# r and k in three buffers loaded apart from v, conv_w later, w_sg's rows in the places of w_val and w_out2, one order for all batches

## The chip, the cores and the metric

The kernel runs on one core of a Trainium2 chip. The metric is the device time in microseconds (us) of one execution. The core has five engines that follow their own instruction streams and meet at semaphores: PE (TensorE: matmuls), ACT (ScalarE), DVE (VectorE), POOL (GpSimd) and SP (SyncE, which here issues every DMA). A DMA that SP issues waits in SP's stream for what it needs, and what stands behind it in the stream waits with it.

## The reference

Three stages, all in float32, for 4 batches of 768 tokens:

```python
# attention: 8 heads of 48, a recurrence over the 768 tokens
cur = einsum('bhd,bhe->bhde', u * kt, vt)
y[:, :, t] = einsum('bhd,bhde->bhe', rt, state + cur)
state = w * state + einsum('bhd,bhe->bhde', kt, vt)
# x: (4, 768, 384), the heads side by side
h = gelu_tanh(x @ w_in)              # 1024 columns: u (512) and v (512)
v_n = layernorm(v) * g_ln
v_s = einsum('ts,bsd->btd', w_sg, v_n) + b_sg   # over all tokens of a batch
x = x + (u * v_s) @ w_out
gate = sigmoid(causal_conv(x, conv_w))          # 5 taps
out = (gate * (x @ w_val)) @ w_out2
```

w_in, w_out, w_val, w_out2 and conv_w come as float64 and are turned into float32 on the chip.

## The kernel before

**Attention by chunks.** The 24 chunks (4 batches of 6) have 128 tokens each. For chunk i the generators give PE these tasks: T (att_T: transposes of r and of k scaled, L515), S (att_S: the scores, L536), K (att_KV: keys by values into the state, L558), Y (att_Y: transposes of dv, then state and scores into y, L591, L598, L603). Around them POOL forms dv = r·k (L494), dv·u (L497), k scaled (L475) and v·sum (L499); DVE masks the scores (L544). y goes from PSUM through ACT (x_rows, L616) into one yT buffer, by two DMAs to a scratch xd and by a third back as columns of xf (L626): the transposition into x. x is split into a high and a low part (x_parts, L654 and L658) for each third of a half of 384 tokens in batch 0, for a whole half in the others.

**The MLP tasks.** Each product of 32-bit values is three matmuls (three, L757 to L759: high·high, high·low, low·high). mlp_V(b, i) gives v for 128 tokens (9 matmuls of 512 columns), mlp_U(b, half, f) u for 384 tokens (9 matmuls of 384), mlp_SG the product with w_sg (18 of 384), mlp_O1 that with w_out (12), mlp_VAL that with w_val (9), mlp_O2 that with w_out2 (9). V(b, i) needs its part of x and the upper half of w_in; U(b, half, ·) all of that half of x; SG needs all six V of its batch and one half of w_sg.

**Who sets the order.** A planner in the program itself runs while the program is built. Two lists of generators feed PE, attention and mlp; of attention three tasks are live at a time (WA = 3), of the MLP four (WM = 4): go pulls the next task only when one of the live ones is done, and takes the first live one that is ready. choose prefers attention until its planned PE time reaches A_FIRST + 0.43 of the MLP's. Work for other engines stands in chains (chain): steps with an engine or a choice of engines, a planned duration, the tokens they take and give back, and keys they wait for (after). next_step takes the step that can start first, ties by priority, then by its end. The result is a fixed order on each engine; the durations only serve the planning. Where PE has nothing to do before 130 us of planned time, go adds small filler matmuls (L170).

**The buffers around the change.** r and k of a chunk have two buffers each (rp, kp), v two. load_chunk (L456) issues the three loads, and chain ("ld", i) lets them go when T, dv, kS, D, KV and Y of chunk i-2 are done, so Y(i-2) sets the time. The ring R has NR = 13 tiles: parts of x take three tiles per half, w_sg's six rows one each (prepare_sg), a weight that is being converted one (prepare; at most NW = 3 at once), the parts of g, x2 and of the last product the rest. prepare turns a float64 weight of 128 rows into a high and a low part: a load, a step on ACT, three on DVE, a copy and a subtraction. w_val and w_out2 have tiles of their own from the start. prepare_sg loads w_sg's rows after chunk 3's load and sums their squares on ACT; scale_w_sg (a matmul of 12 columns, L407, on PE, as a task of the MLP list) gives the scale; parts_sg writes each row's two f16 parts (L436, L444) and turns them with two DMA transposes (L439). The first half of w_sg is rows 0 to 2. load_small (L260) brings g_ln, conv_w (three DMAs, L269) and b_sg after chunk 4's load.

**The MLP's order.** For b = 0, mlp (L932) lists V(0..5), scale, then U(0,d) and U(1,d) in turn, SG(0,0..3). For the other batches it lists V(i), U(0,i) in turn and then U(1,d), SG(0,d) in turn.

Of the kernel before, what the change touches and what calls it, by code (L numbers as in the profile page):

```python
# [30 lines left out]
class Kern:  # L31
# [180 lines left out]
    def consts(self):  # L212
# [15 lines left out]
        self.rp = [self.const([P, H, 64], F32, f"rp{i}") for i in range(2)]  # L228
        self.kp = [self.const([P, H, D], F32, f"kp{i}") for i in range(2)]
# [110 lines left out]
    def prepare(self, key, rows, hi, lo, prio, after=()):  # L340
# [15 lines left out]
        def parts(f):  # L356
            return f.rearrange("p (c n) -> p c n", c=hi.shape[1]) if len(hi.shape) == 3 else f
# [42 lines left out]
    def scale_w_sg(self):  # L400
# [63 lines left out]
    def att_new(self, i):  # L464
# [717 lines left out]
```

## Time and profile before

| | us |
|---|---|
| median of 3 runs | 492.62 (490.49 to 495.46) |
| the profiled execution | 496.19 |
| its span, first to last instruction | 494.4 |
| PE busy (share of the span) | 468.7 (95%) |
| DVE busy | 348.5 (70%) |
| ACT busy | 208.3 (42%) |
| POOL busy | 175.2 (35%) |

The mean granted clock of PE over the span is 0.971 of full speed. Matmuls are pipelined and the profile models their ends, so a row's duration is longer than the distance to the next one; the pace is read from starts. The page's chain that ended last gives PE 82% of the span, DVE 5%, POOL 4%, ACT 3%, DMA 2% and 3% to waits for nothing that the profile shows.

### The profile page before, as it was taken

What the parts mean: (1) busy time and instruction counts of PE and PEld (TensorE: products, weight loads), DVE (VectorE), ACT (ScalarE), POOL (GpSimd) and SP (SyncE); (2) the same over time, 40 slices, a digit from 0 to 9 for tenths busy, and PEclk for the clock granted to TensorE, in tenths of its full rate; (3) what the DMA queues carried; (4) which work ended last, traced back from release to release, by engine and by line L of the source; (5) the groups of instructions that cost most, each with busy time, mean ns of one, the idle gap of its engine ahead of it and who ended that gap; (6) DMA issues with size and microseconds to landing.
All of it is one profiled execution on the core that took longest, in us unless ns stands there. A gap on an engine that the chain in (4) does not pass through costs nothing.

```text
span 494.4 us, 9195 instructions
## 1 busy us (share of the span) xinstructions
PE 468.7 (95%) x3550; PEld 392.1 (79%) x3550; DVE 348.5 (70%) x699; ACT 208.3 (42%) x447; POOL 175.2 (35%) x202
## 2 busy tenths in 40 slices
PE   6798797799999999999999999999999999999996
PEld 6677585597777998877788899887787888877796
DVE  5987778966798583656588587467469694667992
ACT  3547856562363435542343163634205165312232
POOL 6766467373014223654244335446101011400000
PEclk9978988899999999999999999999999999999999
DMA  8859985992301434331231451431000301000002
GB/s 158 234 126 285 200 219 123 156 213 68 81 1 50 95 72 122 81 80 34 49 65 42 120 128 34 113 80 34 2 1 16 98 16 49 0 2 0 1 33 70
DMA packets 116274, 41.39 MB, mean 84 GB/s; under 512 B 89344, under 2 KB 114048, under 8 KB 116224
## 3 DMA queue, kind: packets, MB, share of 16 engines
q1 hardware_dynamic: 116224, 40.73, 34.9%
q8 instruction: 30, 0.49, 0.4%
q14 instruction: 20, 0.16, 0.1%
HBM read 28.92 MB, written 9.44 MB: 78 GB/s over the span
## 4 chain that ended last, share of the span: by engine, by line
PE 82%; DVE 5%; POOL 4%; issue 3%; ACT 3%; DMA 2%; SPq 0%; DVEq 0%; POOLq 0%; ACTq 0%
PE pm L757 22%; PE pm L759 20%; PE pm L758 20%; PE pa L603 5%; PE pa L536 4%; PE pa L515 3%; PE pa L598 3%; PE pa L591 2%; PE pa L558 2%; POOL dv L499 1%; DVE sc L544 1%; POOL dv L494 1%; ACT junk L386 1%; DMA wsg<-psg 1%; POOL ks L475 1%
## 5 line engine op out<-in xcount | busy, mean ns | idle before, releaser
L757 PE MATMUL pm<-wsg,vh 128*128 128x384 f16 x192 | 62.9, 328 | 0.0
L759 PE MATMUL pm<-wsg,vh 128*128 128x384 f16 x192 | 62.6, 326 | 0.0
L758 PE MATMUL pm<-wsg,vh 128*128 128x384 f16 x192 | 62.6, 326 | 0.0
L876 DVE SCALAR_TENSOR_TENSOR S<-xf,cw,S 128x384 f32<-128x384 f32 x96 | 59.5, 639 | 2.5 <-ACT S L874 2.1
L844 DVE SCALAR_TENSOR_TENSOR S<-pm,gs,b_bc 128x384 f32<-128x384 f32 x32 | 19.7, 616 | 30.7 <-PE pm L759 30.6
L499 POOL TENSOR_TENSOR dv<-v,dd 128x384 f32<-128x384 f32 x24 | 26.3, 1094 | 39.5 <-DVE dd L492 39.4
L544 DVE TENSOR_TENSOR sc<-pa,mask 128x512 f32<-128x512 f32 x48 | 31.3, 684 | 12.6 <-PE pa L536 10.8
L908 POOL TENSOR_TENSOR R<-S,R 128x384 fp32r<-128x384 f32 x9 | 9.3, 1036 | 78.5 <-ACT R L1110 60.2
L573 ACT ACTIVATE T<-T,W 112x112 f32<-112x112 f32 x80 | 26.8, 380 | 20.5 <-DVE T L567 20.1
L536 PE MATMUL pa<-rT,kT 48*128 48x128 f32 x384 | 29.4, 295 | 5.9 <-ACT kT L521 3.7
L757 PE MATMUL pm<-R,win 128*128 128x384 f32 x96 | 34.9, 363 | 0.0
L757 PE MATMUL pm<-R,wout 128*128 128x384 f32 x96 | 34.2, 357 | 0.0
L536 PEld LDWEIGHTS pa<-rT,kT 48*128 48x128 f32 x384 | 24.7, 196 | 11.7 <-ACT kT L521 5.3
L757 PE MATMUL pm<-win,R 128*128 128x512 f32 x72 | 31.3, 434 | 1.9 <-ACT R L654 1.9
L783 POOL TENSOR_TENSOR rs<-rs,exps 128x1 f32<-128x1 f32 x24 | 14.0, 582 | 53.2 <-DVE rs L780 53.2
L1110 ACT CAST R<-S 128x384 fp32r<-128x384 f32 x30 | 15.4, 513 | 40.4 <-DVE S L846 23.8
L759 PE MATMUL pm<-R,win 128*128 128x384 f32 x96 | 32.3, 337 | 0.0
L759 PE MATMUL pm<-R,wout 128*128 128x384 f32 x96 | 32.3, 336 | 0.0
L758 PE MATMUL pm<-R,wout 128*128 128x384 f32 x96 | 32.3, 336 | 0.0
L758 PE MATMUL pm<-R,win 128*128 128x384 f32 x96 | 32.2, 336 | 0.0
L494 POOL TENSOR_TENSOR dv<-rp,kp 128x384 f32<-128x384 f32 x24 | 25.8, 1073 | 18.1 <-DMA kp<-in_k_dram 14.5
L796 DVE BATCH_NORM_STATS2 bst<-A 128x6 f32<-128x512 f32 x24 | 16.6, 691 | 21.0 <-ACT A L795 21.0
(166 smaller groups left out, 1254.9 us busy)
## 6 DMA issues: line engine op xcount, KB each, us to landing
rp<-in_r_dram SPq DMA_DIRECT2D x24, 192.0 KB, 3.8
kp<-in_k_dram SPq DMA_DIRECT2D x24, 192.0 KB, 3.8
v<-in_v_dram SPq DMA_DIRECT2D x24, 192.0 KB, 2.7
xd<-yT SPq DMA_DIRECT2D x48, 96.0 KB, 2.3
xf<-xd SPq DMA_DIRECT2D x24, 192.0 KB, 2.7
out_dram<-S SPq DMA_DIRECT2D x24, 192.0 KB, 2.1
Rst<-in_moe_w_in_dram SPq DMA_DIRECT2D x8, 384.0 KB, 5.2
Rst<-in_moe_w_out_dram SPq DMA_DIRECT2D x7, 384.0 KB, 5.2
```

The costliest lines, as they stand in the source:

```text
L494: self.chain(("dv", i), ("P", 956.0, lambda e: e.tensor_mul(dv, rp, kp)), after=[("ld", i)] + ([("dT", i - 2)] if i > 1 else []), prio=pr(i))
L499: ("P", 788.0, lambda e: e.tensor_mul(dv, self.vt[i], x["dd"].unsqueeze(2).to_broadcast([P, H, D]))),
L536: nc.tensor.matmul(ps[:, p * P:(p + 1) * P], kT[r0:r0 + D, p, :], rT[r0:r0 + D, p, :], start=True, stop=True)
L544: e.tensor_mul(t, ps.rearrange("s (p t) -> s p t", t=P), mb)
L573: return lambda e: e.activation(tnew[:, p, :], tnew[:, p, :], AF.Copy, scale=self.W[:, p:p + 1])
L603: nc.tensor.matmul(py[r0:r0 + D, p * P:(p + 1) * P], self.vt[i][:, 2 * p + j, :], sc[j][:, p, :], start=False, stop=p == NP - 1)
L757: nc.tensor.matmul(ps, lh, rh, start=m == 0, stop=False)
L758: nc.tensor.matmul(ps, lh, rl, start=False, stop=False)
L759: nc.tensor.matmul(ps, ll, rh, start=False, stop=m == total - 1)
L796: ("V", 602.0, lambda e: e.bn_stats(st, ge)),
L844: ("V", 529.0, lambda e: e.scalar_tensor_tensor(t, pg[:, :TH], self.gs[:, d:d + 1], self.b_bc[:, ts], ALU.mult, ALU.add), [], ["pm"]),
L876: eng.scalar_tensor_tensor(x["t"], row[:, j:j + TH], self.cw[:, e, j:j + 1], x["t"], ALU.mult, ALU.add)
```

## The change

- r and k have NL = 3 buffers each. Their loads are a chain of their own, ("ld", i), that waits for T, dv and kS of chunk i-3; v's load is the chain ("lv", i), which waits for D and Y of chunk i-2 (NV = 2). att_T waits in addition for ("dT", i-2).
- conv_w's three loads leave load_small and become load_conv, after chunk 8's load (AFTER_CW) and after small, with a planned issue time of 12 x 475 ns.
- w_sg's rows are loaded into two tiles with the tags w_val and w_out2 (three rows each) and take no R tile. w_val's and w_out2's tiles are taken from the same places, and their conversions wait for ("w_sg", 0) and ("w_sg", 1), the two halves of w_sg.
- NR goes from 13 to 12, and the split of the second half of x of batch b waits for VAL(b-1) to be done (b > 0).
- mlp lists batch 0 as the others, with scale between the V and the U(1,d).
- The planner counts a DMA transpose as 650 + 1150 ns instead of 1275 + 672.

The diff, without renamings and the parts that only pass a function in place of tiles:

```diff
-                self.dma = max(self.dma, s + (1275 if ns[0] == "T" else 650)) + ns[1]
+                self.dma = max(self.dma, s + 650) + ns[1]
...
-        self.rp = [self.const([P, H, 64], F32, f"rp{i}") for i in range(2)]
-        self.kp = [self.const([P, H, D], F32, f"kp{i}") for i in range(2)]
+        self.rp = [self.const([P, H, 64], F32, f"rp{i}") for i in range(NL)]
+        self.kp = [self.const([P, H, D], F32, f"kp{i}") for i in range(NL)]
...
+    def load_conv(self):
+        nc = self.nc
+        with nc.allow_non_contiguous_dma("per-channel vectors"):
+            for e in range(NC):
+                src = self.conv_w[:, e * P:(e + 1) * P].bitcast(I32).rearrange("k (p two) -> p k two", two=2)
+                nc.sync.dma_start(self.cwd[:, e], src)
...
+        st = [self.wp.tile([P, 3, S], F32, tag=n, name=self.nm("st"), bufs=1) for n in ("w_val", "w_out2")]
+
         def load(i):
-            t = self.st_sg[i] = self.Rst(F32)
-            return lambda e: e.dma_start(t, self.w_sg[i * P:(i + 1) * P, :])
+            self.st_sg[i] = st[i // 3][:, i % 3, :]
+            return lambda e: e.dma_start(self.st_sg[i], self.w_sg[i * P:(i + 1) * P, :])
...
-                ("Q", (1, 1090), lambda e, i=i: load(i)(e), ["R"]),
+                ("Q", (1, 1090), load(i)),
...
-            ("V", Two(930.0), lambda e: ..., [], ["R"]),
-            ("Q", ("T", 672), turn(0)), ("Q", ("T", 672), turn(1), [], ["R"]),
+            ("V", Two(930.0), lambda e: ...),
+            ("Q", ("T", 1150), turn(0)), ("Q", ("T", 1150), turn(1), [], ["R"]),
...
-        for w, t, n, name in ((self.w_out, self.wout, ND, "w_out"), (self.w_val, self.wval, NC, "w_val"), (self.w_out2, self.wo2, NC, "w_out2")):
-            for i in range(n):
-                self.prepare((name, i), w[i * P:(i + 1) * P, :].bitcast(I32), t[0][:, i, :], t[1][:, i, :], prio)
+        def late(name, i):
+            if name not in self.late:
+                t = self.wp.tile([P, 2, NC, DM], F32R, tag=name, name=self.nm(name), bufs=1)
+                self.late[name] = t[:, 0], t[:, 1]
+            return [w[:, i, :] for w in self.late[name]]
+
+        for i in range(ND):
+            self.prepare(("w_out", i), ..., prio)
+        for n, (name, w) in enumerate((("w_val", self.w_val), ("w_out2", self.w_out2))):
+            for i in range(NC):
+                self.prepare((name, i), ..., lambda i=i, name=name: late(name, i), prio, after=[("w_sg", n)])
...
-        old = [(k, i - 2) for k in ("T", "dv", "kS", "D", "KV", "Y") if i >= 2]
-        old = [k for k in old if k[1] % NCH != NCH - 1 or k[0] != "KV"]
+        old = [(k, i - NL) for k in ("T", "dv", "kS") if i >= NL]
+        oldv = [(k, i - NV) for k in ("D", "Y") if i >= NV]
         if i:
-            self.chain(("ld", i), ("Q", (3, 3270), lambda e: self.load_chunk(i, e)), after=old, prio=pr(i))
+            self.chain(("ld", i), ("Q", (2, 2180), lambda e: self.load_chunk(i, e, "rk")), after=old, prio=pr(i))
+            self.chain(("lv", i), ("Q", (1, 1090), lambda e: self.load_chunk(i, e, "v")), after=oldv, prio=pr(i))
...
-            yield 430, [("ld", i) if not n else ("kS", i) if i else "k0"], ["pa"]
+            yield 430, [("ld", i) if not n else ("kS", i) if i else "k0"] + ([("dT", i - 2)] if i > 1 else []), ["pa"]
...
-                    after=[("y", b, 3 * half + 2)], prio=0,
+                    after=[("y", b, 3 * half + 2)] + ([("VAL", b - 1)] if half and b != "g" else []), prio=0,
...
+        for i in range(NCH):
+            out += [V(i)] + ([U(0, i)] if i < ND else [])
         if b == 0:
-            out += [V(i) for i in range(NCH)]
             out.append(self.scale_w_sg())
-            for d in range(ND):
-                out += [U(0, d), U(1, d)]
-            out += [SG(0, 0), SG(0, 1)]
-            out += [SG(0, 2), SG(0, 3)]
-        else:
-            for i in range(NCH):
-                out += [V(i)] + ([U(0, i)] if i < ND else [])
-            for d in range(ND):
-                out += [U(1, d), SG(0, d)]
+        for d in range(ND):
+            out += [U(1, d), SG(0, d)]
...
-        self.load_chunk(0, nc.sync)
+        self.load_chunk(0, nc.sync, "rkv")
...
-        self.chain("small", ("Q", (5, 2150), lambda e: self.load_small()), prio=2, after=[("ld", AFTER_SM)] if AFTER_SM else [])
+        self.chain("small", ("Q", (2, 1300), lambda e: self.load_small()), prio=2, after=[("ld", AFTER_SM)])
+        self.chain("conv", ("Q", (12, 1100), lambda e: self.load_conv()), prio=2, after=[("ld", AFTER_CW), "small"])
...
-AFTER_SG, AFTER_SM = 3, 4
+AFTER_SG, AFTER_SM, AFTER_CW = 3, 4, 8
...
-NR, NS, NA, NX, NY, NPA = 13, 10, 3, 3, 1, 4
+NR, NS, NA, NX, NY, NL, NV, NPA = 12, 10, 3, 3, 1, 3, 2, 4
```

## Rows read from the trace of the kernel before

**Rows 1.** Window table: stretch, length, PE, PEld, DVE, ACT, POOL, clock, DMA, GB/s

```profile
53.85:69.50 15.65, 11.64 (x122) 10.18 (x121) 11.07 (x21) 8.44 (x21) 10.94 (x12) 0.78 1.02 233
69.50:93.30 23.80, 18.49 (x201) 14.98 (x195) 20.89 (x40) 15.81 (x34) 14.35 (x13) 0.93 0.72 143
93.30:115.90 22.60, 21.40 (x103) 19.22 (x104) 17.03 (x36) 11.89 (x28) 11.95 (x14) 0.85 0.86 191
9.50:115.90 106.40, 89.56 (x830) 75.95 (x831) 85.07 (x168) 63.05 (x154) 65.53 (x62) 0.87 0.84 194
115.90:400.00 284.10, 284.10 (x2156) 234.70 (x2154) 193.54 (x380) 109.72 (x231) 94.55 (x104) 1.00 0.26 61
400.00:494.40 94.40, 88.53 (x495) 75.14 (x493) 64.47 (x130) 32.60 (x57) 10.39 (x16) 0.99 0.06 20
```

**Rows 2.** Window table of L170, the filler matmuls: PE, PEld, clock, DMA, GB/s

```profile
53.85:93.30 39.45, 6.59 (x77) 5.04 (x77) 0.87 0.84 179
```

**Rows 3.** Timeline of PE: start, us, operation, count, idle before and its releaser

```profile
57.54 0.62 PE L515 MATMUL pa<-ident,rp 128*112 128x128 f32 x4 [1.79 <-DMA rp<-in_r_dram]
...
69.53 0.50 PE L757 MATMUL pm<-win,R 128*128 128x512 f32 x1
...
71.72 0.18 PE L407 MATMUL pm<-ssb,onesb 128*128 128x12 bf16 x1
...
93.30 0.50 PE L757 MATMUL pm<-win,R 128*128 128x512 f32 x1 [1.91 <-ACT R L654]
...
95.83 0.63 PE L757 MATMUL pm<-win,R 128*128 128x512 f32 x1
...
103.65 0.34 PE L757 MATMUL pm<-R,win 128*128 128x384 f32 x1
...
114.40 0.34 PE L759 MATMUL pm<-R,win 128*128 128x384 f32 x1
...
115.88 0.33 PE L757 MATMUL pm<-wsg,vh 128*128 128x384 f16 x1
...
403.42 0.40 PE L757 MATMUL pm<-win,R 128*128 128x512 f32 x1
```

**Rows 4.** Timeline of SP's queue: start, us to issue, line, transfer, count

```profile
40.19 2.55 SPq L382 DMA_DIRECT2D Rst<-in_moe_w_sg_dram  x5
...
45.79 5.07 SPq L269 DMA_DIRECT2D cwd<-in_moe_conv_w_dram  x3
...
51.75 1.22 SPq L620 DMA_DIRECT2D xd<-yT  x1
...
53.57 0.43 SPq L462 DMA_DIRECT2D rp<-in_r_dram  x1
...
60.51 0.87 SPq L626 DMA_DIRECT2D xf<-xd  x1
...
90.60 3.88 SPq L439 DMA_TRANSPOSE wsg<-psg  x3
...
107.21 1.54 SPq L346 DMA_DIRECT2D Rst<-in_moe_w_out_dram  x3
```

**Rows 5.** Timeline of ACT: a copy out, and the late split of x

```profile
43.43 0.56 ACT L616 COPY yT<-pa 112x512 f32<-112x512 f32 x1
...
92.97 0.68 ACT L654 CAST R<-xf 128x128 fp32r<-128x128 f32 x3
```

**Rows 6.** DMA view, issues: transfer, count, median us from issue to landing

```profile
wsg<-psg SPq DMA_TRANSPOSE x12, 3.0
```

**Rows 7.** Timeline of POOL: first product of chunk 5

```profile
58.34 1.17 POOL L494 TENSOR_TENSOR dv<-rp,kp 128x384 f32<-128x384 f32 x1
```

**Rows 8.** Chain that ended last, 389 to 410 us: a split of x

```profile
395.03 0.51 ACT R L654
```

**Rows 9.** Tile wval: PE's matmuls, count, ns min/median/max, first and last start

```profile
L757 PE MATMUL pm<-R,wval x72: 333/338/476, 143.5 to 483.1; 128*128 128x384 f32 x72
```

**Rows 10.** Waits of SP's queue: total us, times, longest us

```profile
SPq L462 <- PE pa L603: 153.9, 18, 23.9
```

More of the change, by code (lines that the diff above doesn't have):

```diff
@@ L263, in load_small @@
         self.cw = self.const([P, NC, KC], F32, "cw")
-        self.cwd = cwd = self.const([P, NC, KC, 2], I32, "cwd")
+        self.cwd = self.const([P, NC, KC, 2], I32, "cwd")
         with nc.allow_non_contiguous_dma("per-channel vectors"):
             nc.sync.dma_start(self.g, self.g_ln.rearrange("(f p) -> p f", p=P))
-            for e in range(NC):
-                src = self.conv_w[:, e * P:(e + 1) * P].bitcast(I32).rearrange("k (p two) -> p k two", two=2)
-                nc.sync.dma_start(cwd[:, e], src)
         self.b_bc = self.const([P, S], F32, "b_bc")
@@ L338, in from_double, with prepare @@
         ]
-    def prepare(self, key, rows, hi, lo, prio, after=()):
+    def prepare(self, key, rows, dst, prio, after=()):
         x = {}
@@ L354, in step, with high @@
             x["steps"].pop(0)(e)
-        def parts(f):
-            return f.rearrange("p (c n) -> p c n", c=hi.shape[1]) if len(hi.shape) == 3 else f
+        def high(e):
+            hi, lo = x["d"] = dst()
+            if len(hi.shape) == 3:
+                x["f"] = x["f"].rearrange("p (c n) -> p c n", c=hi.shape[1])
+            e.copy(hi, x["f"]) if hasattr(e, "copy") else e.tensor_copy(hi, x["f"])
         self.chain(
@@ L457, in load_chunk @@
+        for i in range(ND):
+            self.prepare(("w_out", i), self.w_out[i * P:(i + 1) * P, :].bitcast(I32), lambda i=i: [w[:, i, :] for w in self.wout], prio)
+        for n, (name, w) in enumerate((("w_val", self.w_val), ("w_out2", self.w_out2))):
+            for i in range(NC):
+                self.prepare((name, i), w[i * P:(i + 1) * P, :].bitcast(I32), lambda i=i, name=name: late(name, i), prio, after=[("w_sg", n)])
+    def load_chunk(self, i, e, which):
         b, c = divmod(i, NCH)
-        rp, kp = self.rp[i % 2], self.kp[i % 2]
@@ L894, in mlp_VAL @@
             x = self.x2[half, d]
-            self.three(pv[:, :TH], (self.wval[0][:, d, cs], self.wval[1][:, d, cs], x[0], x[1]), (d, NC))
+            self.three(pv[:, :TH], (*(w[:, d, cs] for w in self.late["w_val"]), x[0], x[1]), (d, NC))
         if e == NC - 1:
             self.give("R", NC)
+            if half:
+                self.mark(("VAL", b))
         hi, lo = self.gv[half, e] = self.R()
@@ L919, in mlp_O2 @@
             g = self.gv[half, e]
-            self.three(po[:, :DM], (g[0][:, cs], g[1][:, cs], self.wo2[0][:, e, :], self.wo2[1][:, e, :]), (e, NC))
+            self.three(po[:, :DM], (g[0][:, cs], g[1][:, cs], *(w[:, e, :] for w in self.late["w_out2"])), (e, NC))
         if q == 2:
@@ L1051, in run @@
         self.wout = [self.const([P, ND, DM], F32R, f"wout{i}") for i in range(2)]
-        self.wval = [self.const([P, NC, DM], F32R, f"wval{i}") for i in range(2)]
-        self.wo2 = [self.const([P, NC, DM], F32R, f"wo2{i}") for i in range(2)]
+        self.late = {}
         self.load_w()
         self.consts()
-        self.load_chunk(0, nc.sync)
+        self.load_chunk(0, nc.sync, "rkv")
         self.load_u()
```

32 lines of the change are left out of this document (17 added, 15 removed).

## The prediction

> **What bounds the kernel now.** I read the window table by stage first [rows 1]. From 115.9 to 400 us PE's rows fill the stretch (284.10 of 284.10 us) at full clock, 2.4 GHz: there the time is PE's own work, which the change leaves alone (every matmul keeps its shape and count). From 400 to the end PE is busy 88.53 of 94.40 us. What can be lost or won lies before 115.9: from 9.5 to 115.9 PE is busy 89.56 of 106.40 us at a mean granted clock of 0.87, and part of even that is filler. In the 39.45 us from 53.85 to 93.30 PE is busy 11.64 + 18.49 = 30.13 us, of which 6.59 are L170's filler [rows 1, 2]; real work is 23.5 us, so 15.9 us of the stretch go unused.
>
> Next, PE's timeline says why [rows 3]. Chunk 5's first transposes at 57.54 wait for rp's load. V(0,2) runs at 69.53, the one matmul of scale_w_sg at 71.72, and then PE has no MLP work until V(0,3) at 93.30, which waited for ACT's split of x (L654). Between the two stands one U task, U(0,0). So at 93.30 three V and one U of batch 0 are done; V(0,3..5) and seven U follow, and the first SG matmul is at 115.88. From 93.30 on PE lacks nothing.
>
> Why was U(0,1), whose inputs are those of U(0,0), not done at 73? The window: four tasks may be live, and after scale the list before goes U(0,0), U(1,0). Live were then V(0,3), V(0,4), V(0,5) and U(1,0), all four of which need the second half of x. And why was x's fourth part split only at 92.97 [rows 5]? It needs three R buffers at once; of 13, three hold x's first half, six w_sg's rows, and up to three a weight being converted.
>
> **The change, part by part.** The sum is made against the profiled execution: 496.19 us, span 494.4, 1.8 around it. That execution lies 3.6 us above the median of the runs shown (492.62); I take the same difference off the median. 1%, some 4.9 us, is about what a measurement of this kernel can tell from no change.
>
> *Order of batch 0, and w_sg's rows out of the R ring* (one answer). The work from 93.30 to 115.88 is: V(0,3..5), 27 matmuls of 512 columns, at the pace of V(0,2)'s nine (69.53 to 71.72: 2.19 us) 6.6 us; seven U, 63 matmuls, which run from 103.65 to 114.40 at 0.173 us each [rows 3], 10.9 us; from the last of them to 115.88 attention's transposes, 1.3 us. That is 18.8 of 22.58 us; the other 3.8 are the waits at 93.30 and half the clock after them: a V matmul's row reads 0.63 us at 95.83 against 0.40 at 403.42, the levels 1.2 and 2.4 GHz. With the new order U(0,1..3) stand right behind V(0,2), 4.7 us of work. With nine R buffers left beside x's first half instead of four, x's fourth and fifth parts no longer wait for w_sg. So the 17.5 us of V and U fit into the 15.9 unused us before 93.30 and the few after.
>
> SG then waits for w_sg. Its first half is six DMA transposes; the last two of these head the group of three at 90.60, 1.29 us each to issue, hence are issued by 93.2 [rows 4], and land a median 3.0 us later [rows 6]: 96.2. I take the first SG matmul at 97 in place of 115.88: 18.9 us.
>
> The scale of w_sg moves the other way: it is now eleventh in the list and enters the window once seven of the ten before it are done (V(0,0..2) and U(0,0..3)), so three U, 4.7 us, come ahead of it. Against this stands the next part.
>
> *conv_w later.* SP's three conv_w loads take 5.07 us to issue from 45.79, with chunk 2's write of y behind them, issued at 51.75 [rows 4] although ACT had copied it out by 43.99 [rows 5]. Without them it goes at up to 5.07 us sooner, and with it x's third part, V(0,2) and scale. Gain 0 to 5.1; I take 4.7, which cancels the later scale. They come back after chunk 8's load, among the transposes: cost 0 to 5.1, since a transpose behind them is late by as much; I take 1, because the planner gives them the lowest priority and an issue time (5.7 us) that keeps them out of a busy queue.
>
> *r and k in three buffers, v apart.* As many DMAs as before. Before, chunk i's r and k waited for Y(i-2); now for uses of chunk i-3. Chunk 5's rp was issued at 53.57 [rows 4] and its first product ran on POOL at 58.34 [rows 7]. The load can now be issued before the w_sg loads at 40.19, some 13 us sooner, and what it saves reaches the sum only through x's sixth part and scale: a gain of 0 to 10; I take 0, the SG start above being set by w_sg, and keep the rest for a rival. At the start v of chunk 1 and r, k of chunk 2 go ahead of weights: three issues of 0.43 to 1 us like those at 53.57, a cost of 0 to 3; I take 1.
>
> *w_val and w_out2 converted after the halves of w_sg.* Before, w_out2's loads were issued at 107.21 [rows 4], w_val's earlier. The first matmul that reads w_val is at 143.5 [rows 9], 27.6 us after the first SG. That is the cover; a cost of 0 if conversion starts as w_sg's half is done, and I take 0. If the cover is gone it is up to 25: see the slower rival. Six conversions fewer before SG may also gain there, 0 to 10 us of DVE and DMA; this too is a rival's.
>
> *x's second half behind the last VAL of the batch before; twelve R buffers.* In the last batch that split ran at 395.03 [rows 8]; now it follows the last VAL, which ends where V(3,0) begins, 403.42 [rows 3]. Ahead of V(3,3) come three O2, three V and three U, 4.7 + 6.6 + 4.7 = 16 us of PE: cover enough for one split, but no attention is left there to fill a gap. 0 to 4; I take 2 for both.
>
> Sum: 18.9 - 1 - 1 - 2 = 14.9. Profiled 496.2 - 14.9 = 481.3; on the median **478**.
>
> **A rule weighed.** From 53.85 to 69.50 the DMA share reads 1.02 at 233 GB/s [rows 1]. The Trainium skill (DMA: Bandwidth & Descriptors, section "Issuing engines are not separate DMA queues") says that all transfers, whichever engine issues them, run on the same 16 engines and interleave. By it loading earlier adds no bandwidth, it only changes who waits. The trace agrees where the share stands at 1.02. It supports the second rival below.
>
> **The rivals.**
> *Early DVE or DMA sets SG's start.* From 9.5 to 115.9 DVE is busy 85.07 us and the DMA engines 0.84 of 106.4 = 89.4 [rows 1]. If all of it still has to come before SG, at DVE's best stage share (20.89/23.80 = 0.88) SG starts at 9.5 + 85.07/0.88 = 106, at a DMA share of 1 at 99. With 106 the gain is 9.7 - 4 = 6: **487**. For: both are near their limit. Against: w_val's and w_out2's six loads and most of their conversion now come later, so there is less to do before SG.
> *A faster attention as well.* If the early r and k save chunk 5 and those behind it 10 us more, scale and transposes move too: gain 15 + 10 = 25, **468**. Against: the same DVE and DMA totals.
> *No gain.* x's second half is still late (six converted parts take R buffers one by one while x wants three at once), or the transposes take longer next to 4.7 us of U ahead of scale and conv_w among them: 18.9 - 4.7 - 5.1 - 4 = 5 at first, 0 with x late: **491**.
> *Slower.* w_val's loads now come in time behind v loads, and SP's queue stands at a v load until Y(i-2) is done, 153.9 us in 18 waits, the longest 23.9 [rows 10]. Before, the loads of w_val and w_out2 were issued by 108.75 and passed these waits. If w_val's first load falls behind such a wait, 27.6 - 23.9 = 3.7 us of cover remain for landing and conversion, which I estimate at 15 for the three weights (seven steps each, of the 0.6 to 1.2 us of the single steps in rows 5 and 7, partly beside each other): PE lacks 11 us, and as much again for w_out2 behind the next v, and work after a gap runs at the lower clock. 25 lost against 15 won: **502**. It decides once w_val's first load is issued over 12 us after the first SG matmul. Against: attention can fill such a gap, and where PE is ahead SP's waits are only slack.
>
> **How the numbers follow.** Forecast (gain 11 to 20) 0.50; faster attention 0.10; early bound 0.18; no gain 0.13; slower 0.09. Faster by over 1% (below 487.7): 0.50 + 0.10 + most of 0.18 = 0.76; within 1%: 0.15; slower: 0.09. Its own range is 473 to 482; the 8-in-10 range reaches to the fast rival and through the early bound to no gain: 465 to 493.
>
> **What would show it.** Right: U(0,1..3) directly behind V(0,2); V(0,3) at 70 to 80 without a wait for L654; the first SG matmul at 95 to 100; PE full from there; filler between 54 and 93 nearly gone; conv_w's loads after the middle of the transposes. Wrong: the first SG at 105 or later (which releaser stands there tells DVE, DMA or the transposes), PE waiting for w_val or w_out2 after it, or a gap at V(3,3).

## The result, and the profile after

| | us |
|---|---|
| before, beside the change | 493.66 (490.49 to 495.46, 4 runs) |
| changed | 486.88 (485.40 to 488.09, 4 runs) |
| ratio | 0.986, 95% interval 0.9815 to 0.9905 |
| changed, second session beside other runs of before (493.25) | 485.89 (485.32 to 486.87, 6 runs); 0.9859, 0.9812 to 0.9906 |
| profiled execution of the changed kernel, its span | 488.09, 486.4 |

It is faster by 1.4%: 6.8 us by the medians and 8.0 by the spans, where 14.9 had been forecast. The lines of three, L757 to L759 before, are now L778 to L780; rp, kp and v load at L482, w_sg at L392, w_in at L350; yT is filled at L637 and written to xd at L641.

The window table by stage of the changed kernel, in the columns of [rows 1], here also for the stretches ahead of 53.85:

```profile
9.50:32.30 22.80, 16.35 (x213) 14.17 (x215) 14.95 (x28) 11.12 (x29) 18.25 (x16) 0.93 0.95 229
32.30:53.85 21.55, 14.47 (x181) 11.62 (x177) 15.84 (x34) 15.43 (x43) 9.96 (x10) 0.98 0.95 265
53.85:69.50 15.65, 13.83 (x114) 12.24 (x116) 12.74 (x25) 7.68 (x22) 6.57 (x7) 0.81 0.60 128
69.50:93.30 23.80, 23.80 (x172) 21.23 (x172) 20.81 (x53) 17.50 (x38) 15.28 (x20) 1.00 0.44 93
93.30:115.90 22.60, 21.80 (x217) 16.55 (x216) 17.17 (x28) 9.14 (x21) 15.76 (x15) 1.00 0.90 192
115.90:392.00 276.10, 275.89 (x2083) 231.41 (x2082) 205.49 (x389) 119.08 (x246) 86.58 (x95) 1.00 0.29 67
392.00:486.40 94.40, 86.28 (x476) 73.33 (x474) 59.98 (x124) 31.84 (x56) 10.55 (x16) 0.96 0.06 20
```

The same view of the kernel before for the two stretches that [rows 1] left out:

```profile
9.50:32.30 22.80, 17.74 (x215) 14.97 (x215) 18.28 (x36) 10.72 (x27) 19.13 (x14) 0.86 0.76 184
32.30:53.85 21.55, 20.28 (x200) 16.60 (x198) 17.80 (x36) 16.18 (x47) 9.16 (x11) 0.92 0.88 235
```

The reader is to see a gain and a loss. From 69.5 to 93.3 PE is now full at full clock (23.80 of 23.80; before 18.49, filler included). But from 32.3 to 53.85 it is busy 14.47 us where it was busy 20.28.

PE's busy time holds filler and half-clock rows, so I count in another way. From each stretch I take off its matmuls without filler, each kind times its distance from start to start where PE runs through at full clock (0.230 us for 512 columns, 0.175 for 384, 0.163 in SG; attention's groups, for 16: 1.09 at S, 1.01 at Y's last). What is left is PE time **lost** to waits, filler and half clock. It is worked out, not a view. Two profiles of the changed kernel differ by up to 0.5 in a stretch, two of w_sg_late_lead by up to 1.5, and in "rest" (all before 32 and after 200 us) both pairs differ by 3.0 to 3.4. The other kernels have one profile each. All kernels of this study in one table:

| kernel | 32–54 | 54–70 | 70–93 | 93–116 | 116–200 | rest | span |
|---|---|---|---|---|---|---|---|
| before | 5.4 | 9.8 | 10.2 | 3.9 | 1.4 | 31.2 | 494.4 |
| changed | 11.9 | 4.3 | 0.2 | 1.4 | 1.8 | 34.5 | 486.4 |
| changed, second profile | 11.6 | 4.8 | 0.2 | 1.5 | 1.5 | 31.5 | 483.6 |
| sq_late | 11.7 | 2.8 | 0.4 | 4.4 | 3.5 | 33.0 | 488.0 |
| sg_after5 | 7.4 | 4.2 | 1.2 | 5.3 | 3.8 | 32.9 | 487.6 |
| scale_early | 11.6 | 4.7 | 1.5 | 2.4 | 2.4 | 33.8 | 488.8 |
| old_order | 11.6 | 4.6 | 5.1 | 0.2 | 8.1 | 31.0 | 493.3 |
| order_alone | 5.4 | 10.6 | 2.4 | 8.0 | 6.8 | 31.3 | 497.2 |
| rk_after_y2 | 5.5 | 10.0 | 0.6 | 5.4 | 13.0 | 34.9 | 501.4 |
| rk_after_y3 | 4.0 | 7.1 | 1.6 | 2.3 | 10.7 | 32.7 | 491.4 |
| no_val_wait | 12.2 | 4.1 | 0.1 | 1.4 | 1.7 | 32.2 | 484.3 |
| lead_from_5 | 5.4 | 8.8 | 3.3 | 4.1 | 7.2 | 31.8 | 493.3 |
| y2_sg_after2 | 7.3 | 2.9 | 0.6 | 7.9 | 6.0 | 36.0 | 493.2 |
| sg5_scale | 8.0 | 5.5 | 6.8 | 1.9 | 1.7 | 33.0 | 490.0 |
| sg4_scale | 9.7 | 3.8 | 2.2 | 1.6 | 3.2 | 31.5 | 484.4 |
| w_sg_late_lead | 2.7 | 1.8 | 8.6 | 4.1 | 1.0 | 34.3 | 484.9 |
| the same, second profile | 4.2 | 0.8 | 8.0 | 4.1 | 1.2 | 30.9 | 481.8 |
| lead_6_w_sg_early | 8.4 | 2.3 | 2.0 | -0.2 | 6.3 | 32.8 | 484.4 |
| lead_7_w_sg_early | 8.3 | 1.5 | 5.9 | 2.4 | 5.1 | 31.1 | 487.8 |
| lead_8_w_sg_early | 8.7 | 3.1 | 2.6 | 6.7 | 11.7 | 33.4 | 499.1 |

From 54 to 116 us the change saves 23.9 - 5.9 = 18.0 us. From 32 to 54 it loses 6.5 more. The rest costs 3.3 in one profile and 0.3 in the other of the same kernel.

**Where the 6.5 us went.** PE's timeline of the changed kernel; the rows answer to [rows 3]:

```profile
43.65 0.50 PE L778 MATMUL pm<-win,R 128*128 128x512 f32 x1
...
46.59 2.24 PE L170 MATMUL warm<-onesb 128*128 128x128 bf16 x37
55.65 1.07 PE L612 MATMUL pa<-ident,dv 128*112 128x128 f32 x4 [6.82 <-ACT yT L637]
...
83.76 0.18 PE L417 MATMUL pm<-ssb,onesb 128*128 128x12 bf16 x1
...
107.75 0.34 PE L778 MATMUL pm<-wsg,vh 128*128 128x384 f16 x1
...
399.51 0.44 PE L778 MATMUL pm<-w_out,R 128*128 128x384 f32 x1 [2.04 <-DVE S L925]
...
403.27 0.63 PE L778 MATMUL pm<-win,R 128*128 128x512 f32 x1
```

The same view of the kernel before, the first V and the Y task of chunk 3:

```profile
32.28 0.61 PE L757 MATMUL pm<-win,R 128*128 128x512 f32 x1
...
42.63 0.94 PE L591 MATMUL pa<-ident,dv 128*112 128x128 f32 x4 [0.15 <-DVE sc L544]
```

V(0,0) begins at 43.65 instead of 32.28, and chunk 3's Y, at 42.63 before, stands at 55.65 behind 37 fillers and the longest wait of the stretch, 6.82 us for ACT's copy of chunk 2's y (L637). ACT's timeline says why that copy is late (an entry in brackets is the idle time before the row and what ended it):

```profile
48.85 0.55 ACT L338 ACTIVATE S<-Rst 128x384 f32<-128x384 f32 x1 [1.19 <-DMA Rst<-in_moe_w_in_dram]
50.85 0.51 ACT L364 CAST win<-S 128x384 fp32r<-128x384 f32 x1 [1.45 <-DVE S L341]
52.04 0.81 ACT L809 ACTIVATE A<-A,nm,rs 128x512 f32<-128x512 f32 x1 [0.68 <-POOL nm L805]
...
54.06 0.51 ACT L364 CAST win<-S 128x384 fp32r<-128x384 f32 x1 [0.78 <-DVE S L341]
...
54.93 0.57 ACT L637 COPY yT<-pa 112x512 f32<-112x512 f32 x1
```

ACT follows its list, and in it stand steps that turn rows of w_in, each waiting in turn for a load, for DVE, for POOL. The load that row 48.85 waited for is late in SP's queue (start, us to issue):

```profile
24.56 0.39 SPq L482 DMA_DIRECT2D rp<-in_r_dram  x1
...
25.71 2.74 SPq L392 DMA_DIRECT2D st<-in_moe_w_sg_dram  x5
...
35.32 2.36 SPq L482 DMA_DIRECT2D rp<-in_r_dram  x1
37.73 2.72 SPq L482 DMA_DIRECT2D kp<-in_k_dram  x1
40.55 2.19 SPq L482 DMA_DIRECT2D v<-in_v_dram  x1
...
44.27 0.70 SPq L350 DMA_DIRECT2D Rst<-in_moe_w_in_dram  x1
45.07 0.43 SPq L641 DMA_DIRECT2D xd<-yT  x1
...
92.84 5.29 SPq L449 DMA_TRANSPOSE wsg<-psg  x4
```

And before, in the same queue:

```profile
33.04 0.42 SPq L620 DMA_DIRECT2D xd<-yT  x1
...
34.01 0.46 SPq L346 DMA_DIRECT2D Rst<-in_moe_w_in_dram  x1
```

w_in's last row of the early part goes out 10.3 us later, and chunk 1's y 12.0 us later. Ahead of them now stand w_sg's loads (25.71; 40.19 in [rows 4]) and r and k up to chunk 7, where before it was r and k up to chunk 3; chunk 5's r goes out at 24.56 instead of 53.57 [rows 4], 29 us sooner. The DMA engines are busy 0.95 of both early stretches, where it was 0.76 and 0.88.

The rule weighed in the prediction (the Trainium skill, DMA: Bandwidth & Descriptors, "Issuing engines are not separate DMA queues") says that all of these transfers run on the same 16 engines and interleave. The trace agrees: from 32.3 to 53.85 the rate rises from 235 to 265 GB/s and the share from 0.88 to 0.95, so part of the earlier loading fits into time that was idle, and the rest makes others wait.

One thing in this account isn't shown by these rows. The planner makes the order on every engine anew for each version, so a load moved forward changes ACT's list as well as the DMA queue. That the copy stands behind that row of w_in is the planner's doing; the late load makes the place costly.

### The profile page after: what moved, and what is told of

The parts are those of the page before. It is cut to its first block, busy times and chain, and to the rows that moved or that the text cites. A ratio compares the mean times of both kernels' runs of the same rounds, so it can differ in the third digit from the quotient of the medians.

```text
span 486.4 us, 9114 instructions
## 1 busy us (share of the span) xinstructions
PE 458.8 (94%) x3517; PEld 386.7 (80%) x3517; DVE 352.6 (72%) x700; ACT 214.7 (44%) x457; POOL 167.6 (34%) x196
## 4 chain that ended last, share of the span: by engine, by line
PE 83%; DVE 4%; issue 3%; POOL 1%; ACT 1%; DMA 1%; POOLq 0%
PE pm L778 23%; PE pm L779 21%; PE pm L780 21%; PE pa L624 4%; PE pa L557 4%; PE pa L619 4%; PE pa L536 3%; PE pa L612 2%; PE pa L579 1%; DVE S L897 1%; DMA Rst<-in_moe_w_out_dram 1%; DVE psg L454 1%; DVE sc L565 1%; DVE R L679 0%; DVE S L925 0%
## 5 line engine op out<-in xcount | busy, mean ns | idle before, releaser
L897 DVE SCALAR_TENSOR_TENSOR S<-xf,cw,S 128x384 f32<-128x384 f32 x96 | 61.1, 653 | 4.0 <-ACT S L895 3.4
L778 PE MATMUL pm<-wsg,vh 128*128 128x384 f16 x192 | 62.9, 328 | 0.0
L780 PE MATMUL pm<-wsg,vh 128*128 128x384 f16 x192 | 62.6, 326 | 0.0
L565 DVE TENSOR_TENSOR sc<-pa,mask 128x512 f32<-128x512 f32 x48 | 31.3, 684 | 17.2 <-PE pa L557 14.2
L515 POOL TENSOR_TENSOR dv<-rp,kp 128x384 f32<-128x384 f32 x24 | 27.5, 1145 | 32.1 <-PE pa L612 27.3
L520 POOL TENSOR_TENSOR dv<-v,dd 128x384 f32<-128x384 f32 x24 | 24.3, 1014 | 36.0 <-DVE dd L513 33.5
L778 PE MATMUL pm<-R,win 128*128 128x384 f32 x96 | 34.8, 363 | 0.0
L496 POOL TENSOR_TENSOR ks<-kp,tabS 128x384 f32<-128x384 f32 x24 | 26.9, 1120 | 21.4 <-PE pa L579 10.2
L1127 ACT CAST R<-S 128x384 fp32r<-128x384 f32 x33 | 16.9, 514 | 39.0 <-DVE S L867 19.3
L778 PE MATMUL pm<-R,wout 128*128 128x384 f32 x96 | 34.1, 355 | 0.0
L779 PE MATMUL pm<-R,wout 128*128 128x384 f32 x96 | 32.3, 337 | 0.0
L780 PE MATMUL pm<-R,wout 128*128 128x384 f32 x96 | 32.3, 337 | 0.0
L780 PE MATMUL pm<-R,win 128*128 128x384 f32 x96 | 32.3, 337 | 0.0
L779 PE MATMUL pm<-R,win 128*128 128x384 f32 x96 | 32.3, 337 | 0.0
L594 ACT ACTIVATE T<-T,W 112x112 f32<-112x112 f32 x80 | 27.0, 382 | 11.8 <-DVE T L588 11.7
L835 ACT ACTIVATE S<-pm 128x384 f32<-128x384 f32 x32 | 15.6, 488 | 35.7 <-PE pm L780 34.6
L557 PE MATMUL pa<-rT,kT 48*128 48x128 f32 x384 | 27.9, 285 | 2.5 <-DVE kT L544 1.4
L557 PEld LDWEIGHTS pa<-rT,kT 48*128 48x128 f32 x384 | 23.3, 187 | 7.8 <-issue 4.0
```

Source lines behind the costliest of these rows:

```text
L496: e.tensor_mul(t[:, :, 0:D], kp, self.tabS)
L515: self.chain(("dv", i), ("P", 956.0, lambda e: e.tensor_mul(dv, rp, kp)), after=[("ld", i)] + ([("dT", i - 2)] if i > 1 else []), prio=pr(i))
L520: ("P", 788.0, lambda e: e.tensor_mul(dv, self.vt[i], x["dd"].unsqueeze(2).to_broadcast([P, H, D]))),
L557: nc.tensor.matmul(ps[:, p * P:(p + 1) * P], kT[r0:r0 + D, p, :], rT[r0:r0 + D, p, :], start=True, stop=True)
L565: e.tensor_mul(t, ps.rearrange("s (p t) -> s p t", t=P), mb)
L594: return lambda e: e.activation(tnew[:, p, :], tnew[:, p, :], AF.Copy, scale=self.W[:, p:p + 1])
```

## The experiments

Kernels are the changed one with the edit shown, unless said otherwise. Ratios are to the kernel before, run beside it. The expectations name theories by letters and spell them out. The **lead** of r and k is that they are let go before Y(i-2) is done, as in the changed kernel.

**sq_late: ACT's squares of w_sg's rows out of the way of yT.** The loads of w_sg stay as early; the squares wait for chunk 1's y.

```diff
-    prio=prio, after=[("ld", AFTER_SG)],
+    prio=prio, after=[("w_sg_ld", i), ("y", 0, 1)],
```

> The changed kernel with one edit: w_sg's rows are loaded as early as there (after chunk 3's r and k), but ACT squares them only when chunk 1's y has been read back. Theory A (the squares stand ahead of chunk 1's copy out of PSUM on ACT and hold it, the one yT buffer passes the delay on, PE waits 6.8 us at 55.65): PE's long wait before chunk 3's Y goes, V(0,0) starts at 32 to 38 us instead of 43.65, the time falls by 4 to 8 us, to 479 to 483. Theory B (the early loads fill the DMA engines, 0.95 from 9.5 to 54, and everything early is late by that): V(0,0) stays at 42 or later, 485 to 489. Theory C (the scale of w_sg, at 83.76 in place of 71.72, sets the gain): no earlier first SG matmul than 107, 485 to 489.

489.78 us (ratio 0.9893, 0.986 to 0.9926). The wait before Y(3) is still 5.76 us and 32 to 54 loses 11.7. ACT's squares aren't the cause: theory A falls, and the time lies just above the 485 to 489 of the other two.

**sg_after5 and scale_early: w_sg's loads later; the scale earlier.**

```diff
-AFTER_SG, AFTER_SM, AFTER_CW = 3, 4, 8
+AFTER_SG, AFTER_SM, AFTER_CW = 5, 4, 8
```

> The changed kernel with w_sg's loads let go after chunk 5's r and k instead of chunk 3's: loads and squares both come later. Theories A and B both expect V(0,0) at 32 to 38 and a time of 478 to 483; A and B are told apart by the run with late squares alone. Theory C: 485 to 489, the first SG matmul at 105 or later.

```diff
-        if b == 0:
-            out.append(self.scale_w_sg())
+            if b == 0 and i == 1:
+                out.append(self.scale_w_sg())
```

> The changed kernel with the scale task third to fifth in the list (behind V(0,1) and U(0,1)) in place of eleventh, so that the transposes of w_sg can start before V(0,2..5). Theory C: the first SG matmul moves from 107.75 to 95 to 100 and the time falls by as much as 8 us, to 479 to 483. Theory A: PE has work without a gap from 55.65 on anyway (attention fills), so SG comes earlier, attention later, and the time stays at 484 to 489.

sg_after5: 491.44 (0.9928, 0.99 to 0.9955), where theories A and B had expected 478 to 483. The wait for yT shrinks to 0.4 us and 32 to 54 loses 7.4, but SG starts at 116.0 and 93 to 200 loses 9.1 instead of 3.2. scale_early: 490.43 (0.9904, 0.9877 to 0.9932). PE's timeline of scale_early, the first SG matmul:

```profile
88.90 0.34 PE L778 MATMUL pm<-wsg,vh 128*128 128x384 f16 x1
```

SG starts 18.9 us earlier than in the changed kernel and nothing is gained. What counts is whether PE has any ready work; where SG isn't ready, V, U and attention fill the time.

**old_order and order_alone: the order of batch 0, and only that.** old_order puts the list of before back into the changed kernel; order_alone puts the new list into the kernel before.

```diff
+            out += [V(i) for i in range(NCH)]
+            out.append(self.scale_w_sg())
+            for d in range(ND):
+                out += [U(0, d), U(1, d)]
+            out += [SG(0, d) for d in range(ND)]
```

> The changed kernel with batch 0's MLP listed as before the change (V(0..5), scale, then U(0,d) and U(1,d) in turn, SG). The prediction's step: three U tasks and V(0,3..5) then no longer fill the time before SG, PE shows filler or waits between 70 and 100 us, and the time rises by 5 to 12 us over the changed kernel, to 492 to 499. If w_sg's rows outside the ring R alone gave the fill, it stays within 3 us of the changed kernel, 484 to 490.

> The kernel before with batch 0's MLP in the new order and nothing else. The prediction's step: with w_sg's rows still in the ring R, x's fourth part waits for R buffers until the transposes are done, so only U(0,1..3), 4.7 us, move ahead and scale comes later by as much: 488 to 496, within 1% of before. If the order alone gives the fill: 482 to 487.

old_order: 497.34 (1.0053, 1.003 to 1.0075), 10.5 us over the changed kernel's median (9.5 by the ratios, as the sessions differ) and 6.9 over its span in the profile; there 4.9 more are lost from 70 to 93 and 6.3 from 116 to 200, and some 4 less elsewhere. order_alone: 497.26 (1.004, 1.0002 to 1.0079): 70 to 93 loses 7.8 less, 93 to 200 loses 9.5 more. So the order is needed and by itself worth nothing: it pays only together with other parts. Which of them it takes wasn't tried one by one; the lead isn't it, since rk_after_y2, without it, loses 0.6 from 70 to 93.

**rk_after_y2 and rk_after_y3: the lead of r and k taken back.** r and k still have three buffers, but wait for Y(i-2) as before, or for Y(i-3).

```diff
-        old = [(k, i - NL) for k in ("T", "dv", "kS") if i >= NL]
+        old = [(k, i - NL) for k in ("T", "dv", "kS") if i >= NL] + ([("Y", i - 2)] if i >= 2 else [])
```

> The changed kernel, three buffers kept, but r and k of chunk i are let go only when Y(i-2) is done, as before the change; with chunk 3's load w_sg's loads move back too. Theory D (the loads that three buffers let go early stand ahead of chunk 1's write of y, of w_in's last rows and of x in SP's queue and on the DMA engines, and cost the 6.5 us that PE loses more from 32 to 54 than before): V(0,0) at 32 to 38, PE's lost time from 32 to 54 back to 5 to 8 us, the time 478 to 483. If the loss comes from the planner's other order and not from these loads: V(0,0) at 42 or later, 485 to 490.

> The changed kernel, three buffers kept, r and k of chunk i let go when Y(i-3) is done in addition to T, dv and kS: one chunk of lead in place of what the queue allows. Theory D: between the two, PE's lost time from 32 to 54 at 6 to 10 us, the time 480 to 486. Otherwise 485 to 490.

rk_after_y2: 503.97 (1.0182, 1.0103 to 1.0261), against theory D's 478 to 483. The stretch 32 to 54 loses 5.5, as before the change, V(0,0) is at 32.0 and the long wait is gone; 54 to 70 loses 10.0 and 116 to 200 loses 13.0. rk_after_y3: 492.87 (0.9955, 0.9914 to 0.9995), against 480 to 486; the same three stretches lose 4.0, 7.1 and 10.7. Theory D is right about 32 to 54 in the first run and too high in the second (6 to 10 expected), and wrong about the time in both. But since w_sg's loads wait for chunk 3's, they moved as well, to 38.83 in the first run and to 20.29, ahead of the changed kernel's 25.71, in the second: each run changes two things, and I first read them as one.

**no_val_wait: the split of x's second half in the last batch doesn't wait for VAL.**

```diff
-    ([("VAL", b - 1)] if half and b != "g" else [])
+    ([("VAL", b - 1)] if half and b != "g" and b != B - 1 else [])
```

> The changed kernel without the wait of x's second half in the last batch for the VAL tasks of the batch before. The prediction charged up to 4 us to this wait where no attention is left: PE's wait of 2.04 us at 399.5 and the half clock after it go, the time falls by 1 to 3 us, to 484 to 487. If the wait at 399.5 stands for a product of batch 2 (its row names S at L925) and not for x, nothing changes: 486 to 489.

485.49 (0.9813, 0.9731 to 0.9894): not to be told from the changed kernel. PE's waits in the last 100 us (total us, times, longest) are still headed by the one for L925 that stands at 399.51 in the changed kernel; it halves:

```profile
PE pm L778 <- DVE S L925: 1.1, 1, 1.1
PE pm L778 <- ACT A L816: 0.4, 1, 0.4
```

**lead_from_5, y2_sg_after2, w_sg_late_lead: the two early loadings apart.** The first keeps the lead from chunk 5 on (w_sg's loads, behind chunk 3's, fall back to 40 us); the second has no lead, but w_sg's loads behind chunk 2's; the third has the lead, and w_sg's loads behind chunk 7's.

```diff
+ ... + ([("Y", i - 2)] if 2 <= i < 5 else [])      # lead_from_5
+ ... + ([("Y", i - 2)] if i >= 2 else [])          # y2_sg_after2, and AFTER_SG = 2
+AFTER_SG, AFTER_SM, AFTER_CW = 7, 4, 8             # w_sg_late_lead
```

> The changed kernel, except that r and k of chunks 2 to 4 wait for Y(i-2) as before; from chunk 5 on they have their lead. Theory E (the early loads of chunks 2 to 4 and of w_sg, on full DMA engines, push w_in and chunk 1's y back and cost the 6.5 us more that PE loses from 32 to 54; the lead of chunk 5's r and k is what gains 54 to 70): V(0,0) near 32, PE loses about 5.5 from 32 to 54 and 4 to 6 from 54 to 70, and the time is 480 to 485 if the rest stays as in the changed kernel. Rival P (whatever is moved at the start, the loads that PE then lacks are late elsewhere): 32 to 54 falls to 5.5, but 54 to 70 rises to 8 to 10 or 116 to 200 loses 8 or more, and the time is 488 or above.

> All r and k wait for Y(i-2) as before, and w_sg's loads go out after chunk 2's r and k instead of chunk 3's. It tells which of the early loads costs the stretch from 32 to 54. If w_sg's six loads alone do it: PE loses 9 to 12 from 32 to 54 and V(0,0) is at 38 or later. If it is the lead of r and k: 5 to 6, V(0,0) at 32 to 34. In both cases 54 to 70 loses about 10, since r and k have no lead; the time is 495 to 505.

> The changed kernel with w_sg's loads after chunk 7's r and k, with the lead of r and k for all chunks. It is the fourth corner of a table of two by two: lead and early w_sg (the changed kernel: PE loses 11.9 us from 32 to 54 and 4.3 from 54 to 70), no lead and late w_sg (5.5 and 10.0), no lead and early w_sg (7.3 and 2.9). Theory F (the place of w_sg's loads sets 54 to 70, the lead costs 32 to 54 some 4.6): with w_sg's loads at 40 us or later, 54 to 70 loses 8 to 10 and 32 to 54 about 9 to 10; the time is 490 or above. Rival (the lead gains 54 to 70): 3 to 5 lost there.

lead_from_5: 494.09 (1.0011, 0.9971 to 1.0051), against my theory E's 480 to 485. y2_sg_after2: 496.42 (1.0043, 1.0 to 1.0085), within the 495 to 505 expected, but with 7.3 lost from 32 to 54, between the two branches, and 2.9 instead of about 10 from 54 to 70. w_sg_late_lead: 485.69 (0.979, 0.9732 to 0.9849), where my theory F expected 490 or more, and 9 to 10 lost from 32 to 54. The table of two by two, lost from 32 to 54, from 54 to 70, from 70 to 93 and from 93 to 200:

| | w_sg's loads at 38 to 51 us | at 22 to 31 us |
|---|---|---|
| no lead | 5.5, 10.0, 0.6, 18.4 (rk_after_y2) | 7.3, 2.9, 0.6, 13.9 (y2_sg_after2) |
| lead | 2.7, 1.8, 8.6, 5.1 (w_sg_late_lead) | 11.9, 4.3, 0.2, 3.2 (changed) |

Either loading alone gains from 32 to 70 (15.5 lost without both, 10.2 and 4.5 with one); both together lose it again, 16.2. And the lead is what keeps 93 to 200 cheap. The other kernels bear out the first column of the large table: the five with both loadings early (changed, sq_late, scale_early, old_order, no_val_wait) lose 11.6 to 12.2 from 32 to 54, the four that load w_sg and r and k of chunks 2 to 4 about as late as before the change (before, order_alone, rk_after_y2, lead_from_5) 5.4 to 5.5. With the lead and w_sg's loads behind chunk 3's, 4's, 5's and 7's r and k it is 11.9, 9.7, 7.4 to 8.0 and 2.7 to 4.2. rk_after_y3, where w_sg's loads go out from 20.29 on and chunk 5's r only at 38.06, so that the two are apart as well, loses 4.0. The windows of w_sg_late_lead from 32.3 on:

```profile
32.30:53.85 21.55, 20.96 (x226) 17.25 (x223) 16.44 (x36) 13.56 (x41) 12.65 (x14) 0.97 0.86 233
53.85:69.50 15.65, 14.84 (x118) 12.75 (x118) 12.81 (x36) 14.28 (x38) 10.20 (x12) 1.00 0.86 195
69.50:93.30 23.80, 19.50 (x179) 16.45 (x181) 23.07 (x43) 14.94 (x36) 13.75 (x15) 0.86 0.86 158
```

SP's queue and ACT's copy in the same kernel (two views):

```profile
34.65 0.37 SPq L482 DMA_DIRECT2D rp<-in_r_dram  x1
35.07 0.58 SPq L482 DMA_DIRECT2D kp<-in_k_dram  x1
35.74 0.84 SPq L641 DMA_DIRECT2D xd<-yT  x1
...
37.72 0.39 SPq L482 DMA_DIRECT2D v<-in_v_dram  x1
...
43.96 1.20 SPq L392 DMA_DIRECT2D st<-in_moe_w_sg_dram  x2
...
57.73 1.54 SPq L350 DMA_DIRECT2D Rst<-in_moe_w_in_dram  x1
```

```profile
46.42 0.59 ACT L637 COPY yT<-pa 112x512 f32<-112x512 f32 x1 [2.48 <-PE pa L536]
```

Chunk 1's y goes out at 35.74 instead of 45.07, chunk 2's y is copied at 46.42 instead of 54.93, and PE is busy 20.96 us from 32 to 54. The loads of r, k (chunk 6) and v (chunk 4), which in the changed kernel took 2.36, 2.72 and 2.19 us to issue behind w_sg's, take 0.37, 0.58 and 0.39 here. w_in's last row goes out at 57.73, later than in the changed kernel, and does no harm, since here the copy of chunk 2's y doesn't stand behind it in ACT's list. So the lateness of that row alone isn't the cause.

The bill comes at 69.5: there DVE is busy 23.07 of 23.80 us, and PE loses 8.6. In this kernel the chain that ended last runs through DVE from 69.35 to 84.24, over the low parts of x (L679) and of w_sg (L454):

```profile
74.51 3.05 DVE R L679 x3
...
79.98 2.79 DVE psg L454 x3
```

**lead_6, lead_7 and lead_8, w_sg early: from which chunk the lead pays.** As y2_sg_after2 (w_sg behind chunk 2's r and k), with the lead from chunk 6, 7 or 8 on.

```diff
+ ... + ([("Y", i - 2)] if 2 <= i < 6 else [])      # 7, 8
+AFTER_SG, AFTER_SM, AFTER_CW = 2, 4, 8
```

> w_sg's loads after chunk 2's r and k; r and k of chunks 2 to 5 wait for Y(i-2) as before, from chunk 6 on they have their lead. Theory F (the lead costs only while the DMA engines are full, and pays after 93, where the run without any lead lost 13.9 us): 32 to 54 loses 7 to 8, 54 to 93 3 to 5, 93 to 200 3 to 6: some 44 to 47 lost in all, a time of 478 to 483. Rival (what is lost later is lost whatever the lead, by w_out2's last load behind a wait of SP's queue): 93 to 200 loses 11 to 14, 490 to 496.

> As the run before with the lead from chunk 7 on. Theory F: 32 to 93 loses 10 to 12 and 93 to 200 3 to 7, 478 to 484. Rival: 93 to 200 loses 11 to 14, 490 to 496.

> As the run before with the lead from chunk 8 on. Theory F: 32 to 93 loses 10 to 12; chunks 6 and 7, whose r and k then come as late as without a lead, may still lose 2 to 4 from 70 to 116, 480 to 487. Rival: 93 to 200 loses 11 to 14, 490 to 496.

485.43 (0.9789, 0.9733 to 0.9846), 492.35 (0.9938, 0.9901 to 0.9975) and 499.19 (1.0061, 1.0021 to 1.01): the later the lead begins, the more is lost from 93 on (6.1, 7.5, 18.4). The direction is theory F's, that the lead pays after 93; but none of its times is reached (478 to 483, 478 to 484, 480 to 487): lead_7 has the rival's, and lead_8 lies above both. In lead_8 w_out2's last load is issued at 141.67, and PE's timeline has the longest wait of its stretch:

```profile
163.46 0.48 PE L778 MATMUL pm<-wsg,vh 128*128 128x384 f16 x1 [5.43 <-DVE S L925]
```

The chain that ended last, of lead_8 (start, us, what), shows what DVE did just ahead of L925:

```profile
160.25 0.53 DVE S L897
160.78 1.10 DVE w_out L372
161.88 1.06 DVE S L897 x2
162.94 0.48 DVE S L925
```

A late step of w_out2 (w_out in this kernel's names) stands in the chain. That is a small instance of the prediction's slower rival. Of the eight kernels whose last w_out2 load is issued between 132 and 142 us, seven (old_order, both rk_after, lead_from_5, y2_sg_after2, lead_6, lead_8) lose 6.0 to 13.0 from 116 to 200. But the eighth, sg_after5, at 140.33, loses 3.8, and order_alone, at 115.30, loses 6.8: this is a pattern and no more.

**sg5_scale and sg4_scale: both remedies at once,** w_sg's loads behind chunk 5's or 4's r and k, and the scale early; the edits are those of sg_after5 and scale_early.

> The changed kernel with w_sg's loads after chunk 5's r and k (PE lost 7.4 us from 32 to 54 in that run, but 5.3 from 116 to 140 with SG at 116) and scale after V(0,1) and U(0,1). Theory E: 7 to 8 lost from 32 to 54, SG earlier than 116, 116 to 140 loses under 3, the time 483 to 487. Rival P: the loss comes back after 54, the time is 488 to 492, as with either edit alone.

> As the run before with w_sg's loads after chunk 4's r and k. Theory E: between the changed kernel's 11.9 and 7.4 lost from 32 to 54, the rest as in the run before, 484 to 488. Rival P: 488 to 492.

490.86 (0.9924, 0.9883 to 0.9964) and 486.77 (0.9849, 0.978 to 0.9919). The first is rival P's: 32 to 54 gains 3.9 and 70 to 93 gives back 6.6. The second is the changed kernel's time.

**The best version beside the changed kernel,** in one session, 6 runs each.

> The changed kernel itself, beside the next run on the same chip. Ratio to the kernel before 0.981 to 0.991, a time of 485 to 489; PE loses 11 to 12 us from 32 to 54.

> w_sg's loads after chunk 7's r and k, all else as changed. If keeping the two loadings apart is worth something, the time is 2 us or more under the run before, outside both intervals; if the loss only moves (2.7 instead of 11.9 from 32 to 54, but 12.7 instead of 1.6 from 70 to 116), the two lie within 2 us of each other.

485.89 (485.32 to 486.87) against 483.40 (482.22 to 484.21): no run of the one lies among the other's. w_sg's loads moved behind chunk 7's r and k are worth 2.5 us, the first of the two outcomes, a ratio to the kernel before of 0.9797 (0.975 to 0.9844) instead of 0.9859. The ratios' intervals overlap, since the runs of before spread from 490.13 to 498.48; by the runs side by side it beats both kernels.

## Why the prediction was wrong

**Right: the waits that it read.** The stretch 54 to 116 us was to lose some 18.9 us less, and loses 18.0 less. No filler stands between 53.85 and 93.30 any more (6.59 us before, [rows 2]); V and U of batch 0 run through from 69.5 to 93.3; conv_w's loads went out at 65.92 and held nobody up. old_order and order_alone show that the order and other parts are needed together, which fits the prediction's "one answer". That 18.0 came so near 18.9 is partly luck: 18.9 was reckoned as the way by which SG's start would move, and that moved by 8.1.

**Wrong without cost: SG's start as the measure.** I forecast 97; it is 107.75. The scale runs at 83.76, not about 72, so the transposes begin at 92.84, hardly earlier than needed. It cost nothing, and scale_early, with SG at 88.90, gained nothing. Nor did chunk 2's y come 4.7 us sooner without conv_w ahead of it, the gain that was to cancel the later scale: it is copied out only at 54.93, where before it was written at 51.75 [rows 4].

**The step that failed: "r and k in three buffers, v apart", costed at 0 with 1 us at the start, and the unspoken assumption that the stretch ahead of 53.85 stays as it is.** I saw that chunk 5's r and k move 13 us forward and asked what they gain, not whom they push back; they moved 29. They and the loads of chunks 4, 6 and 7 went in front of w_in's last rows and of chunk 1's y, at a time when the DMA engines were busy 0.88 already, together with w_sg's loads, which the same edit brought forward because they are tied to chunk 3's. Measured: 6.5 us more lost from 32 to 54 (0.4 more from 9.5 to 32). The two by two shows that it is the coincidence of the two loadings that costs: with the lead alone the stretch loses 2.7 (4.2 in a second profile). By which way it costs, the full queue or the other order that the planner then gives ACT, wasn't separated.

**The tail.** 2 us were set aside. The wait at 399.51 is 2.04 us, where before there were waits of 1.1, 0.2 and 0.2 (half a microsecond more), and in the first profile half-clock rows follow it (0.63 at 403.27 against 0.40 in [rows 3]). The second profile of the same kernel, PE's timeline, has the same wait without them:

```profile
400.03 0.45 PE L778 MATMUL pm<-w_out,R 128*128 128x384 f32 x1 [2.04 <-DVE S L925]
...
402.75 0.39 PE L778 MATMUL pm<-win,R 128*128 128x512 f32 x1
```

The fifteen matmuls from the wait's end to the next V take 3.76 us in the first profile and 2.72 in the second. Where the half clock comes it costs 1 us and more; the term was of the right size or too dear. Another 1.7 us of "rest" in the first profile are the program's end, below.

**The sum with what was measured:** 18.0 - 6.5 - 3.3, and 0.4 lost more from 116 to 200, is 7.8, to the rounding the span's gain of 8.0; in the second profile it is 17.4 - 6.2 - 0.3 - 0.1 = 10.8, its span's gain. The 6.5 are the larger part of the 6.9 that lack to 14.9 in the first profile; in the second, 4.1 lack and the 6.2 are more than that. What differs between the two profiles, 3.0 in "rest" for the most part, is no matter of the change. Yet moving loads gave the 6.5 back in no version tried: w_sg_late_lead takes 9.2 us out of 32 to 54 (2.7 instead of 11.9) and loses 11.1 more from 70 to 116; from 32 to 116 it loses 17.2 where the changed kernel loses 17.8. Six versions lie between 17.1 and 18.1 there, and only lead_6 (12.5) and rk_after_y3 (15.0) below, which lose 6.3 and 10.7 from 116 to 200; the rest lie above, at 18.7 to 26.4.

**The rivals.** "Early DVE or DMA" named 487 and SG at 106; 486.88 and 107.75 came. Its mechanism as put, that SG's start is set by the work ahead of it and sets the time, falls with scale_early, so its 487 came out by luck. Its core, that the early part has little room however the loads stand, fits the 17 to 18 us above and the 23.07 us of DVE in 23.80, but not lead_6's 12.5; whether there is such a floor, and what sets it, wasn't separated from the planner's order and stays open. "Slower" didn't come in the changed kernel (w_val's first matmul at 130.1, no wait for it), but in variants with late w_out2 something like it did.

## What to carry to other kernels

When a buffer is added so that loads run ahead, list what stands behind them in the issuing queue and whose engine waits in order for that; here, in a stretch with a DMA share of 0.88 before the change, earlier loads made others later. Two moves that each gain can cost when they land in the same stretch, so test them in a table of two by two before naming one of them. And count the work of the bounding engine by stretch rather than following one milestone: a start 19 us earlier was worth nothing where other work filled the gap.

## What the runs showed of the hardware

- A DMA's issue on SP is not of one length: in the changed kernel the load of one chunk's r, 192 KB, took 0.39 us at 24.56 and 2.36 at 35.32, both in stretches with a DMA share of 0.95, so the mean share alone doesn't tell. The long one came behind w_sg's loads; in w_sg_late_lead, without them, it took 0.37 at 34.65. Everything behind a long issue in the queue is late by it.
- The same wait of 2.04 us was followed by half clock in one execution of the changed kernel and by full clock in another (the mean granted clock from 392 to 410 us is 0.91 and 1.00). A half-clock row behind a wait is not a fixed price of that wait.
- The end of the program varies between runs of one kernel. The last copy to S ends 3.8 us ahead of the span's end in the second profile of the changed kernel and 5.5 ahead in the first (ACT's timeline, second profile first):

```profile
479.34 0.48 ACT L951 COPY S<-pm 128x384 f32<-128x384 f32 x1 [1.08 <-PE pm L780]
```

```profile
480.36 0.48 ACT L951 COPY S<-pm 128x384 f32<-128x384 f32 x1 [1.08 <-PE pm L780]
```

What makes the difference at the end wasn't tried.
